# Keys and queries of the fifth unit turned by DMA, with the order of the work planned anew

## The chip, the cores and the metric

The kernel runs on one core of one Trainium2 chip. The metric is the time of the device in microseconds. The core has five engines that run side by side, each with an order of instructions of its own: TensorE (PE; its loads of weights are shown apart as PEld), VectorE (DVE), ScalarE (ACT), GpSimd (POOL) and SyncE (SP). Transfers run on 16 DMA engines; here nearly all of them are issued by SP, and the weights by POOL.

## The reference

The reference is a gated linear attention, followed by a feed-forward layer with an exact gelu. Batch 4, 8 heads, 768 tokens, 48 numbers a head; the feed-forward part has 3072 tokens, 384 columns and a hidden width of 2048.

```
f = sigmoid(f_logit)
for t in range(S):                       # per batch and head
    state = f[t][:, None] * state + outer(k[t], v[t])      # 48 x 48
    y[t] = q[t] @ state
x = y with heads side by side            # 3072 x 384
out = gelu(x @ w_in) @ w_out             # 384 -> 2048 -> 384
```

## The kernel before

**Tiles.** The tokens are cut into 24 tiles of 128 (n = 0 to 23), six to a batch. Two tiles make a unit (u = 0 to 11, n = 2u and 2u + 1). Units 0 to 4 are pair units: two neighbouring tokens lie on one partition, so that a load's runs are 384 bytes; units 5 to 11 have their tokens one to a partition.

**Attention, one unit.** SP loads the gate logits, k, q and v (L433 for pair units, L441 for others). ACT takes exp and ln of the gates (E and L, L478 and L481). PE sums the logarithms over a tile's tokens (C, L494 to L504), and ACT turns the sums into factors (L509, L511, and L514 or L518 for a whole tile's decay). DVE, in two cases POOL, multiplies k and q with them (L524, tile `sc`), and v is cast to bf16 (L529, on POOL unless the unit is in `HVC`). Then keys and queries have to be turned, so that the 48 numbers of a head lie on the partitions (function `turn`): either PE turns them into a PSUM bank in 8 transposes a tile (L557) and DVE, or ACT for tiles in `HKQ`, copies the bank to `kq` (L563), or, for units in `KDMA`, SP issues one DMA transpose for each tile (L545). PE forms scores (A: L723 in pair units, L661 in others), DVE masks them (L570). PE adds up the state's change (S: L745 or L684), which DVE and POOL carry on from tile to tile (L590, L594, L596, L601), and forms y from scores and from the state (L765, L644, L697, L638). y is cast (L614; ACT for tiles in `HYB`) and turned into x^T, by PE and a copy (L630, L633; ACT for tiles in `HX`) or by a DMA transpose (L618) for units in `XDMA`.

**Feed-forward, one group of 256 tokens, one for each unit.** F1: 48 products with w_in (L801), gelu of 512 columns at a time on ACT (L811); F2: 32 products with w_out, 16 for each of the two tiles, planned in pieces of 4 (L820), then a copy to SBUF (L834, on DVE for tiles in `ODVE`, else on ACT) and a store (L836). exp and ln lie in another table set than gelu, so ACT loads a table at each change between them (L865).

**The order.** Nothing is scheduled by hand or by the hardware across engines: the class `Plan` collects all operations with an expected duration, what they read and write, the buffers they need and a rank, and then places them one by one, always the one that could start first, with equal times (to 0.05 us) going by rank. That gives each engine a fixed order. The rank is 20 for each unit (10 for each tile) plus an offset by kind (`PRI`; feed-forward products come 1000 later), plus a random offset: one of at most 1.0 for all, and one from a generator for each unit, whose seed stands in `SEEDS` and whose width is 0.5, 1, 3 or 8, by the seed's remainder on division by 4. The loads go in the order of `LOADS`, where a letter and a number name one load of a unit (f0: gates of unit 0), u4 all four of unit 4, and i and o pieces of w_in and w_out. Buffers are limited too: four PSUM banks are for F1, F2 and what `EG`, `ET`, `EX` and `EA` put there, four for the attention. Until 30 us PE fills planned gaps with products of a junk tile (L859) that nobody reads.

Of the kernel before, what the change touches and what calls it, by code (L numbers as in the profile page):

```python
# [24 lines left out]

SPREAD, SEED = (1.0, 97)

SEEDS = [0, 3, 358, 3531, 1454, 1223, 983, 3849, 2582, 1403, 2107, 2867]

EAGER = 0.0  # L30

HOLD = 25.0
PRI = {'C': 0, 'T': 1, 'A': 2, 'S': 2.5, 'Y': 3, 'X': 4, 'F': 5}
BANKS = (4, 0, 4)


# [45 lines left out]
class Plan:  # L82
# [30 lines left out]
    def run(self):  # L113
        free = dict.fromkeys(list(LAT), 0.7)
        free["DMA"] = 1.8
        rng = random.Random(SEED)
        own = [random.Random(x) for x in SEEDS]
        for o in self.ops:
            if o.prio > -5:
                k = min(max(int(o.prio % 1000) // 20, 0), len(SEEDS) - 1)  # L120
                o.prio += rng.uniform(-SPREAD, SPREAD)
                if SEEDS[k]:
                    w = (0.5, 1.0, 3.0, 8.0)[SEEDS[k] % 4]
                    o.prio += own[k].uniform(-w, w)
# [84 lines left out]
EG = [0, 1]  # L209
ET = [0, 1]  # L210
EX = [0]
EA = []
SPLIT = []
HVC = []
HKQ = [0, 2]
HYB = [1]
HX = []
GKP, GQP = ([2], [3])
GAM = []
ODVE = [0, 1, 2, 3, 4, 5, 6, 7, 8, 9, 10, 11, 12, 13, 14, 15, 16, 17, 18, 19, 20, 21, 22, 23]  # L220
XDMA = [5, 6, 7, 8, 9, 10, 11]
KDMA = [5, 6, 7, 8, 9, 10, 11]
AJ = [2, 3, 4, 5, 6, 7, 8, 9, 10, 11]
NGT = 4
WARM = 30.0
LOADS = ['f0', 'k0', 'v0', 'q0', 'f1', 'v1', 'k1', 'q1', 'i0', 'k2', 'f2', 'v2', 'q2', 'i1', 'i2', 'i3', 'o0', 'o1', 'o3', 'f3', 'o2', 'k3', 'q3', 'v3', 'u4']
LOADS += [f"u{n}" for n in range(12) if f"u{n}" not in LOADS and f"c{2 * n}" not in LOADS and f"f{n}" not in LOADS]


@with_exitstack  # L230
def kernel(
# [181 lines left out]
    wo_src = moe_w_out.rearrange("(r p j) m -> r p j m", r=4, j=4)  # L413
    for what in LOADS:
        m = int(what[1:])
# [35 lines left out]
    def decays(u):  # L451
# [33 lines left out]
        for j, n in enumerate(ns):  # L485
# [36 lines left out]
            for w, nm, a, b, off in ((0, "kp", "kt", rg, 0), (1, "qp", "qt", gt, 1)):  # L522
# [4 lines left out]
                    port=True, name=f"{nm.upper()}{n}")  # L527
            hv = u in HVC
            P.add("ACT" if hv else "POOL", 0.40 if hv else 0.47, lambda y=y, j=j, hv=hv: (nc.scalar.copy if hv else nc.gpsimd.tensor_copy)(  # L529
# [5 lines left out]
    def copier(act):  # L535
        return nc.scalar.copy if act else nc.vector.tensor_copy

    def turn(u, kq):


        for j in range(2):
            n = 2 * u + j
            sc = X[n]["sc"]
            if u in KDMA:
                P.add("DMA", 1.5, lambda sc=sc, j=j: nc.sync.dma_start_transpose(  # L545
# [6 lines left out]
            def tpv(tp=tp):  # L552
                return tp.t().bitcast(BF16).rearrange("a (i p t) -> a i p t", i=2, p=P2)

            def trans(i, tpv=tpv, sc=sc):
                for p in range(P2):
                    nc.tensor.transpose(tpv()[:, i, p, :], sc.t()[:, i, 2 * p:2 * p + 2, :], ident)  # L557
            P.add("PE", 0.225, lambda trans=trans: trans(0), rd=[("kp", n), "ident"], wr=[("tk", n)],
                  bufs=[tp, sc, kq], prio=pr + PRI["T"], opens=tp, name=f"Tk{n}")
            P.add("PE", 0.225, lambda trans=trans: trans(1), rd=[("qp", n), "ident"], wr=[("tq", n)],  # L560
                  bufs=[tp, sc], prio=pr + PRI["T"], name=f"Tq{n}")
            help_ = n in HKQ
            P.add("ACT" if help_ else "DVE", 0.86 if help_ else 0.61, lambda tpv=tpv, j=j, help_=help_: copier(help_)(  # L563
                kq.t()[:, :, :, j, :].rearrange("a i p t -> a (i p) t"), tpv().rearrange("a i p t -> a (i p) t")),
                  rd=[("tk", n), ("tq", n)], wr=[("kq", n)], bufs=[tp, kq], prio=pr + PRI["T"], name=f"KQ{n}")

    def mask_scores(aps, ams, key, nm, rd, pr, mk, mkey):
        for hh in range(2):
# [3 lines left out]
                mk.unsqueeze(1).to_broadcast([C, P2, C]), ALU.mult),  # L572
                rd=[rd, mkey], wr=[key + (hh,)], bufs=[aps[hh], ams[hh]], prio=pr + PRI["A"], name=nm)

    def carry(n, sp, mm, mmdur, mmrd, mmbufs, first_c):
# [4 lines left out]
        if mm is not None:  # L580
            P.add("PE", mmdur, mm, rd=mmrd, wr=[("sp", n)], bufs=[sp, tn] + mmbufs + ([] if first_c else [rr]),
                  prio=pr + PRI["S"], opens=sp, name=f"S{n}")

        def spf():
            return sp.t()[:, 0:P2 * 96].rearrange("q (p e) -> q p e", p=P2)

        def glb():
            return gl.t()[:, n % 2, :].unsqueeze(2).to_broadcast([C, P2, 2 * D])
        if first_c:
            P.add("DVE", 0.475, lambda: nc.vector.tensor_tensor(tn.t(), spf(), glb(), ALU.mult),  # L590
                  rd=[("sp", n), ("gl", n)], wr=[("tn", n)], bufs=[sp, tn, gl], prio=pr + PRI["S"] - 0.5, name=f"R{n}")
        else:
# [14 lines left out]
    def outputs(n, yp):  # L607
# [4 lines left out]
        yb = U[u]["yb"]  # L612
        help_ = n in HYB
        P.add("ACT" if help_ else "DVE", 0.40 if help_ else 0.475, lambda: copier(help_)(yb.t()[:, i, :], yp.t()[:, 0:HD]),  # L614
# [10 lines left out]
        def xpv():  # L625
            return xp.t().bitcast(BF16)[:, 0:KO * C].rearrange("a (i t) -> a i t", i=KO)
# [4 lines left out]
        P.add("PE", 0.17, xmm, rd=[("yb", n), "ident"], wr=[("xp", n)], bufs=[yb, xp, xT], prio=pr + PRI["X"], opens=xp, name=f"XT{n}")  # L631
        hx = n in HX
        P.add("ACT" if hx else "DVE", 0.39 if hx else 0.27, lambda: copier(hx)(xT.t()[:, j], xpv()),  # L633
# [13 lines left out]
    def attn_nat(u):  # L647
# [3 lines left out]
        for j in range(2):  # L651
# [5 lines left out]
            def amm(j=j, aps=aps):  # L657
                for p in range(P2):
                    for hh in range(2):
                        r = slice(64 * hh, 64 * hh + 64)  # L660
                        nc.tensor.matmul(aps[hh].t()[:, p * C:(p + 1) * C], kq.t()[r, 0, p, j, :], kq.t()[r, 1, p, j, :],  # L661
                                         start=True, stop=True)
            if u in AJ:
                both.append((n, amm, aps, ams))
# [40 lines left out]
    def attn_pair(u):  # L705
# [8 lines left out]
        for jk in range(2):  # L714
            aps = [(s_fh if jk and u in EA else s_ap).new() for _ in range(2)]
            ams.append([s_am.new(), s_am.new()])

            def amm(jk=jk, aps=aps):
                for p in range(P2):
                    for cc in range(2):  # L720
                        for hh in range(2):
                            r, t = slice(64 * hh, 64 * hh + 64), slice(64 * cc, 64 * cc + 64)
                            nc.tensor.matmul(aps[hh].t()[t, p * C:(p + 1) * C].rearrange("a (j t) -> a j t", j=2),  # L723
                                             kq.t()[r, 0, p, jk, t], kq.t()[r, 1, p, :, t], start=True, stop=True)
            if u in AJ:
                both.append((jk, amm, aps, ams[-1]))
# [55 lines left out]
    def ffn_group(g):  # L782
# [31 lines left out]
        for s_ in range(s):  # L814
# [9 lines left out]
            if n == NCH - 1:  # L824
# [7 lines left out]
                continue  # L832
            od = n in ODVE
            P.add("DVE" if od else "ACT", 0.475 if od else 0.40, lambda op=op, osb=osb, od=od: copier(not od)(osb.t(), op.t()[:, 0:d_model]),  # L834
# [64 lines left out]
```

## Time and profile before

The time before is 184.66 us, the median of 3 runs (184.57 to 184.75). The profiled execution has a span of 183.4 us, with a granted TensorE clock of 0.997.

| | |
|---|---|
| PE busy | 173.3 us, 94% of the span |
| ACT busy | 122.0 us, 67% |
| DVE busy | 100.1 us, 55% |
| POOL busy | 55.2 us, 30% |
| F1 products (L801) | 576, 273 ns each from start to modelled end |
| F2 products (L820) | 384, 326 ns each |
| turns of keys and queries on PE (L557) | 80, for five units |
| DMA transposes of keys and queries | 14, for seven units, 3.2 us to landing |
| bytes read and written in HBM | 25.17 MB and 4.72 MB |

Matmuls are pipelined, so that their durations overlap: a matmul's share of PE's time is the distance from its start to the next one's. [...] A wait is named after what ended it.

### The profile page before, as it was taken

The numbers are of one execution on the slowest core, as the hardware profiler recorded it, in microseconds if no ns is written. First come the engines' busy times: TensorE is split into PE (matmuls) and PEld (weight loads), VectorE is DVE, ScalarE is ACT, GpSimd is POOL, SyncE is SP. The second block draws the span as 40 slices with busy tenths as digits, with TensorE's granted clock in tenths as the row PEclk, the third lists the DMA queues.
The fourth block names the chain that finished last, engine by engine and source line by source line (L and its number), as shares of the span: only waits on it lengthen the run. The fifth ranks groups of instructions, "written<-read, shape, count | busy, mean of one in ns | idle before, by whom it ended". The sixth has DMA issues, their size and how long they took to land.

```text
span 183.4 us, 4932 instructions
## 1 busy us (share of the span) xinstructions
PE 173.3 (94%) x2006; PEld 132.8 (72%) x2006; DVE 100.1 (55%) x193; ACT 122.0 (67%) x207; POOL 55.2 (30%) x118
## 2 busy tenths in 40 slices
PE   7687999999999998998999999999999999999991
PEld 2355679865778677977668987689876796998650
DVE  4288830068987698275978507746115896301111
ACT  2763299965487876989759777537899862495100
POOL 7758970005067342104065101160111830000000
PEclk9999999999999999999999999999999999999998
DMA  5999999989999999999899799998992873201021
GB/s 144 261 261 226 267 168 202 191 217 280 269 225 226 184 186 192 192 184 201 157 209 221 180 180 178 195 219 198 183 237 59 173 157 74 58 31 43 17 99 55
DMA packets 104821, 32.09 MB, mean 175 GB/s; under 512 B 99936, under 2 KB 103904, under 8 KB 104800
## 3 DMA queue, kind: packets, MB, share of 16 engines
q1 hardware_dynamic: 102880, 28.55, 72.6%
q0 software_dynamic: 1776, 3.15, 9.6%
q8 instruction: 15, 0.25, 0.5%
q10 hardware_dynamic: 144, 0.10, 0.2%
q14 instruction: 6, 0.05, 0.1%
HBM read 25.17 MB, written 4.72 MB: 163 GB/s over the span
## 4 chain that ended last, share of the span: by engine, by line
PE 66%; DMA 13%; SPq 10%; DVE 4%; ACT 3%; issue 2%; POOL 0%; DVEq 0%
PE ps L820 30%; PE ps L801 26%; DMA fl<-in_f_logit_dram 9%; SPq L433 6%; SPq L441 3%; DMA vt<-in_v_dram 2%; PE ps L661 2%; DMA kt<-in_k_dram 2%; PE ps L697 1%; ACT L865 1%; DVE sc L524 1%; PE ps L638 1%; PE ps L494 1%; ACT fl L478 1%; SPq L836 1%
## 5 line engine op out<-in xcount | busy, mean ns | idle before, releaser
L811 ACT ACTIVATE gT<-ps 128x512 bf16<-128x512 f32 x96 | 57.8, 672 | 20.8 <-PE ps L801 19.0
L801 PE MATMUL ps<-xT,win 128*128 128x256 bf16 x576 | 69.0, 273 | 0.6 <-ACT gT L811 0.6
L820 PE MATMUL ps<-wout,gT 128*128 128x384 bf16 x384 | 69.0, 326 | 0.0
L801 PEld LDWEIGHTS <-win 128*128 128x128 bf16 x576 | 61.3, 114 | 3.1 <-issue 0.7
L820 PEld LDWEIGHTS <-gT 128*128 128x128 bf16 x384 | 35.9, 98 | 20.3
L834 DVE COPY osb<-ps 128x384 f32<-128x384 f32 x23 | 12.6, 553 | 29.0 <-PE ps L820 18.9
L529 POOL CAST vb<-vt 128x384 bf16<-128x384 f32 x24 | 13.3, 566 | 49.5 <-DMA vt<-in_v_dram 49.3
L570 DVE TENSOR_TENSOR am<-ps,mask 128x512 bf16<-128x512 f32 x28 | 17.4, 681 | 11.3 <-PE ps L661 11.3
L524 DVE TENSOR_TENSOR sc<-qt,gt 128x384 bf16<-128x384 f32 x23 | 13.8, 616 | 17.1 <-ACT gt L511 16.6
L596 POOL TENSOR_TENSOR tn<-rr,gl 128x384 f32<-128x384 f32 x16 | 14.5, 904 | 24.9 <-ACT fl L478 14.6
L601 POOL CAST sb<-tn 48x192 bf16<-48x192 f32 x40 | 15.1, 377 | 18.2 <-DVE tn L590 6.8
L865 ACT ACT_TABLE_LOAD x15 | 19.2, 1283 | 0.3
L524 DVE TENSOR_TENSOR sc<-kt,rg 128x384 bf16<-128x384 f32 x23 | 14.4, 633 | 6.6 <-ACT rg L509 6.3
L509 ACT ACTIVATE rg<-ps 128x384 f32<-128x384 f32 x24 | 11.8, 499 | 8.6 <-PE ps L496 4.8
L614 DVE CAST yb<-ps 128x384 bf16<-128x384 f32 x23 | 12.3, 553 | 6.8 <-PE ps L697 3.6
L478 ACT ACTIVATE fl<-fl 128x768 f32<-128x768 f32 x12 | 10.2, 849 | 8.4 <-DMA fl<-in_f_logit_dram 8.3
L511 ACT ACTIVATE gt<-ps 128x384 f32<-128x384 f32 x24 | 11.7, 502 | 3.0 <-PE ps L500 3.0
L570 DVE TENSOR_TENSOR am<-ps,maskp 128x512 bf16<-128x512 f32 x20 | 12.5, 681 | 2.1 <-PE ps L723 2.1
L859 PE MATMUL ps<-junk 128*128 128x512 bf16 (+3 forms) x34 | 9.8, 418 | 1.6 <-POOL junk L851 1.3
L594 DVE TENSOR_TENSOR rr<-ps,tn 128x384 f32<-128x384 f32 x16 | 8.8, 551 | 3.4 <-POOL tn L596 1.2
L481 ACT ACTIVATE lf<-fl 128x768 bf16<-128x768 f32 x12 | 10.1, 845 | 0.3
L557 PE MATMUL ps<-ident,sc 128*128 128x128 bf16 x80 | 6.5, 220 | 1.3 <-POOL sc L524 0.8
(65 smaller groups left out, 122.6 us busy)
## 6 DMA issues: line engine op xcount, KB each, us to landing
out_dram<-osb SPq DMA_DIRECT2D x23, 192.0 KB, 2.9
fl<-in_f_logit_dram SPq DMA_DIRECT2D x14, 192.0 KB, 3.8
kt<-in_k_dram SPq DMA_DIRECT2D x14, 192.0 KB, 3.8
qt<-in_q_dram SPq DMA_DIRECT2D x14, 192.0 KB, 4.1
vt<-in_v_dram SPq DMA_DIRECT2D x14, 192.0 KB, 3.9
fl<-in_f_logit_dram SPq DMA_DIRECT2D x5, 384.0 KB, 5.9
kt<-in_k_dram SPq DMA_DIRECT2D x5, 384.0 KB, 6.3
vt<-in_v_dram SPq DMA_DIRECT2D x5, 384.0 KB, 6.1
```

The costliest lines, as they stand in the source:

```text
L478: nc.scalar.activation(v, v, AF.Exp, scale=-1.0)
L524: P.add("POOL" if pl else "DVE", 0.80 if pl else 0.475, lambda w=w, a=a, b=b, y=y, j=j, pl=pl: (nc.gpsimd if pl else nc.vector).tensor_tensor(
L529: P.add("ACT" if hv else "POOL", 0.40 if hv else 0.47, lambda y=y, j=j, hv=hv: (nc.scalar.copy if hv else nc.gpsimd.tensor_copy)(y["vb"].t ...
L570: P.add("POOL" if pl else "DVE", 1.15 if pl else 0.61, lambda hh=hh, pl=pl: (nc.gpsimd if pl else nc.vector).tensor_tensor(ams[hh].t(), ap ...
L596: P.add("POOL", 0.83, lambda: nc.gpsimd.tensor_tensor(tn.t(), rr.t(), glb(), ALU.mult), rd=[("rr", n), ("gl", n)], wr=[("tn", n)], bufs=[r ...
L601: P.add("POOL", 0.36, lambda hh=hh: nc.gpsimd.tensor_copy(sb.t()[64 * hh:64 * hh + D, :, D * hh:D * hh + D], tn.t()[64 * hh:64 * hh + D, : ...
L614: P.add("ACT" if help_ else "DVE", 0.40 if help_ else 0.475, lambda: copier(help_)(yb.t()[:, i, :], yp.t()[:, 0:HD]), rd=[("yp", n)], wr=[ ...
L801: nc.tensor.matmul(hps.t()[:, i * tok:(i + 1) * tok].rearrange("a (s t) -> a s t", s=s), col(fo)[:, kk, :], xT.t()[:, :, kk, :], start=(kk ...
L811: nc.scalar.activation(to, fr, AF.Gelu)
L820: nc.tensor.matmul(op.t()[:, 0:d_model], gT.t()[:, fo, s_ * C:(s_ + 1) * C], wout[fo // 4][:, fo % 4, :], start=(fo == 0), stop=(fo == FO ...
L834: P.add("DVE" if od else "ACT", 0.475 if od else 0.40, lambda op=op, osb=osb, od=od: copier(not od)(osb.t(), op.t()[:, 0:d_model]), rd=[(" ...
L865: nc.scalar.preload_act_table_set({"exp": "natural_log_exp_and_others", "gelu": "gelu_and_others"}[o.table])
```

## The change

Unit 4, the last of the pair units, joins the units whose keys and queries are turned by DMA (`KDMA`). This takes its 16 transposes from PE and two copies from DVE, and gives SP's queue two DMA transposes more. With it the order is planned anew: new seeds, other offsets by kind (the turns now rank after the scores, and x and y before both), unit 3's v is loaded after all of unit 4's inputs. Several small operations go to other engines: the v casts of unit 1 from POOL to ACT (`HVC`), the key and query copy of tile 6 (`HKQ`), the y cast of tile 5 (`HYB`), the x copy of tile 4 (`HX`) and the output copies of tiles 3, 5 and 15 (no more in `ODVE`) from DVE to ACT. The second scores of unit 0 take banks of the feed-forward part (`EA`), and the scores of unit 9's two tiles are formed apart (`AJ`, L661 in two steps instead of one).

```diff
-SEEDS = [0, 3, 358, 3531, 1454, 1223, 983, 3849, 2582, 1403, 2107, 2867]
+SEEDS = [0, 684, 383, 3363, 2427, 131, 74, 3619, 3555, 1021, 519, 3174]
...
-PRI = {'C': 0, 'T': 1, 'A': 2, 'S': 2.5, 'Y': 3, 'X': 4, 'F': 5}
+PRI = {'C': 0, 'T': 4, 'A': 3, 'S': 3.5, 'Y': 2, 'X': 1, 'F': 5}
...
-EA = []
+EA = [0]
 SPLIT = []
-HVC = []
-HKQ = [0, 2]
-HYB = [1]
-HX = []
+HVC = [1]
+HKQ = [0, 2, 6]
+HYB = [1, 5]
+HX = [4]
...
-ODVE = [0, 1, 2, 3, 4, 5, 6, 7, 8, 9, 10, 11, 12, 13, 14, 15, 16, 17, 18, 19, 20, 21, 22, 23]
+ODVE = [0, 1, 2, 4, 6, 7, 8, 9, 10, 11, 12, 13, 14, 16, 17, 18, 19, 20, 21, 22, 23]
 XDMA = [5, 6, 7, 8, 9, 10, 11]
-KDMA = [5, 6, 7, 8, 9, 10, 11]
-AJ = [2, 3, 4, 5, 6, 7, 8, 9, 10, 11]
+KDMA = [4, 5, 6, 7, 8, 9, 10, 11]
+AJ = [2, 3, 4, 5, 6, 7, 8, 10, 11]
...
-LOADS = ['f0', 'k0', 'v0', 'q0', 'f1', 'v1', 'k1', 'q1', 'i0', 'k2', 'f2', 'v2', 'q2', 'i1', 'i2', 'i3', 'o0', 'o1', 'o3', 'f3', 'o2', 'k3', 'q3', 'v3', 'u4']
+LOADS = ['f0', 'k0', 'v0', 'q0', 'f1', 'v1', 'k1', 'q1', 'i0', 'k2', 'f2', 'v2', 'q2', 'i1', 'i2', 'i3', 'o0', 'o1', 'o3', 'f3', 'o2', 'k3', 'q3', 'u4', 'v3']
```

## The prediction

> **What bounds the kernel now.** I read the page from the top: busy times, slices, the chain, the groups; then the timeline at the places where TensorE (PE) stood still.
>
> ```profile
> PE 173.3 (94%) x2006; PEld 132.8 (72%) x2006; DVE 100.1 (55%) x193; ACT 122.0 (67%) x207; POOL 55.2 (30%) x118
> ...
> PE   7687999999999998998999999999999999999991
> ...
> DMA  5999999989999999999899799998992873201021
> ```
>
> PE is at 9 tenths in nearly every slice after the fourth (about 23 us), the last slice apart. DVE, ACT and POOL are far from full over the whole span. The 16 DMA engines are about 90% busy until slice 30 (some 140 us) and then nearly free. So PE is the bound, with a saturated DMA system beside it for three quarters of the time.
>
> ```profile
> PE ps L820 30%; PE ps L801 26%; DMA fl<-in_f_logit_dram 9%; SPq L433 6%; SPq L441 3%; DMA vt<-in_v_dram 2%; PE ps L661 2%; DMA kt<-in_k_dram 2%; PE ps L697 1%; ACT L865 1%; DVE sc L524 1%; PE ps L638 1%; PE ps L494 1%; ACT fl L478 1%; SPq L836 1%
> ...
> L801 PE MATMUL ps<-xT,win 128*128 128x256 bf16 x576 | 69.0, 273 | 0.6 <-ACT gT L811 0.6
> L820 PE MATMUL ps<-wout,gT 128*128 128x384 bf16 x384 | 69.0, 326 | 0.0
> ...
> L557 PE MATMUL ps<-ident,sc 128*128 128x128 bf16 x80 | 6.5, 220 | 1.3 <-POOL sc L524 0.8 <-DVE sc L524 0.4
> L563 DVE COPY kq<-ps 128x1024 bf16<-128x1024 bf16 x8 | 5.4, 680 | 0.0
> ```
>
> Counted from start to start (ends overlap), a matmul of L801 takes 0.109 us and one of L820 0.162 us: 576 x 0.109 + 384 x 0.162 = 125 us of the 183.4 us span are the feed-forward part, which no edit touches. In the list of the chain, the pieces before 27 us are loads, the third unit's decays and the first gelu; from 27.3 us to 179.6 us they are mostly PE pieces, end to end. The time is therefore: the start until 27 us, all PE work after it, PE's stops, and 3.8 us of tail (last copy and store).
>
> The stops, from gaps between starts after 27 us: 0.28 us at 41.4, 0.20 at 54.3, 0.66 at 72.1 and 0.77 at 82.5, together 1.9; besides these only 0.10 to 0.15 us where PE changes between the 64-row products of the attention and full ones.
>
> ```profile
> 72.76 0.34 PE L630 MATMUL ps<-ident,yb 128*128 128x128 bf16 x3 [0.49 <-DVE yb L614]
> ...
> 80.35 0.85 ACT L478 ACTIVATE fl<-fl 128x768 f32<-128x768 f32 x1 [0.61 <-DMA fl<-in_f_logit_dram]
> 81.21 1.28 ACT L865 ACT_TABLE_LOAD   x1
> 82.51 1.94 ACT L811 ACTIVATE gT<-ps 128x512 bf16<-128x512 f32 x3
> 83.31 0.93 PE L801 MATMUL ps<-xT,win 128*128 128x256 bf16 x7 [0.62 <-ACT gT L811]
> ```
>
> The first stop is an order in which PE comes to a transpose before DVE has copied its source. The second is a load that came 0.61 us late for ACT, whose queue had a gelu behind it, whose bank PE wanted.
>
> And the start:
>
> ```profile
> 22.63 0.85 ACT L478 ACTIVATE fl<-fl 128x768 f32<-128x768 f32 x1 [3.01 <-DMA fl<-in_f_logit_dram]
> ...
> 25.66 2.54 ACT L811 ACTIVATE gT<-ps 128x512 bf16<-128x512 f32 x4
> ```
>
> The first gelu stands behind the third unit's exp and ln, which waited for its gate load.
>
> [...] one transpose of this form is 1024 packets of 256 B which keep the 16 engines 1.39 us, 262 KB / 1.39 us = 190 GB/s. [...]
>
> **The change part by part.**
>
> *Unit 4 turned by DMA.* PE loses 16 transposes (2 token tiles x 8), DVE two copies of 0.68 us, and two PSUM banks are not taken. From the chain:
>
> ```profile
> 39.02 0.45 PE ps L557 x8
> ```
>
> and another 8 at 47.1 took 0.55, so 16 cost PE 0.90 to 1.10 us; I take 0.9. They stood at 53 to 57 us, inside the packed stretch, so this is on the path. Added: two transposes on SP's queue.
>
> ```profile
> 67.02 3.05 SPq L545 DMA_TRANSPOSE kq<-sc  x2
> ...
> kq<-sc SPq DMA_TRANSPOSE x14, 3.2
> ```
>
> Each holds SP 1.3 us and lands 3.2 us after issue; unit 5's pair also made SP wait 1.3 us for its first source. Who waits for the result: unit 4's score products, at 67.9 in the old order, though its operands were copied by 58.0. With sources ready at about 56.3, SP's 2.6 us and 3.2 us to land (the second overlaps), the result is there by about 62: 6 us of slack, so I cost this wait at zero. What is queued behind: SP's loads for units 5 to 7. They come 2 x 1.39 = 2.8 us (DMA time) to 3.9 us (2 x 1.3 of issue plus the wait) later, if nothing else absorbs it. From group 5 on, an x tile is ready 7.7 to 14.6 us before its first L801 product (x5 at about 89.0, used at 96.7; x7 106.9 and 121.5), except the last two groups, planned with 1.3 and 1.9. So a lateness of 3 us costs PE nothing by way of x. By way of ACT it can: at 80.35 ACT stood at a load with gelus behind it. Bounds 0 and 2.8 us; I take 0, because the new order reckons with the two transposes and can put that exp later.
>
> *v of unit 3 behind all of unit 4's loads.* Unit 3's v was cast at 44.9, unit 4's at 50.9. v3 now lands near 50.9, and k4, q4, f4 each one load (about 1.4 us by SP's spacing) sooner. v3's first user, the state product, ran at 51.9, and its scores' use at 62.8. Cost 0 to 1 us; I take 0.
>
> *Copies moved to ACT.* Off DVE: one key/query copy (0.68; ACT's takes 1.01), one y cast (0.55; ACT 0.48), one x copy (0.35), output copies 3, 5 and 15 (0.55 each). With unit 4's two copies DVE loses 1.36 + 0.68 + 0.55 + 0.35 + 1.65 = 4.6 us, 4.0 of it before 90 us. DVE is busy 9.17, 8.59 and 8.52 us of the three stretches of 10 us from 40 to 70, so there it is nearly a bound, and x2 to x4 come only 1.9 to 2.8 us before use. ACT gets some 4.4 us (1.01 + 0.48 + 0.4 + 3 x 0.5 + 2 x 0.5 for unit 1's v casts), where it had 5.08, 7.75 and 7.05 us busy. The copies of 384 columns have no ACT row of this form; between 0.32 (192 columns) and 0.67 (512), I take 0.5. On PE's path neither counts directly; it makes the short stops less likely in that stretch.
>
> *Unit 0's second scores in the other banks, unit 1's v casts on ACT.* Unit 1's second token tile waits on POOL for casts (two, 0.95 us together) before a 1.30 us product, so unit 1's y comes up to 1 us sooner. It does not move the first gelu, pinned behind the gate load at 22.6. PE idled or ran fillers for 1.4 us between the first L801 at 21.0 and 27.1, so more early work mostly becomes more idling. Bounds 0 and 1.4; I take 0.
>
> *Unit 9's joint scores split.* One more change of product form on PE: 0.1 to 0.2 us lost; I take 0.1.
>
> *The new order.* All ranks (turns and scores later, y and x earlier) and random offsets are redrawn. Every wait of 1.9 us is open: bounds from all closed (-1.9) to new ones. I take 0.4 net gain, since the two long ones are accidents of order and lateness, and DVE gets room, while new accidents are as likely as old ones.
>
> Sum: 184.66 - 0.9 + 0.1 - 0.4 = 183.5.
>
> **The rivals.**
>
> *More than that.* PE's stops all close and the start gains: 184.66 - 0.9 + 0.1 - 1.9 - 0.5 = 181.5. For it: DVE's load before 90 us and x and y ranked first; against: the start hangs on the gate load, whose place in the queue is unchanged.
>
> *Given back.* The 0.9 us turns into waits: PE's order is fixed, and what it leaves becomes longer idling at the next gelu or y. 184.66 and nothing gained. For it: gelu pace (0.6 us a piece against 0.65 us of products) lets ACT set the pace in the gelu stretches, and ACT gets 4.4 us more; against: outside the shown stops PE waits for nothing.
>
> *Slower: the load stream is the bound before 90 us.* DMA was 1.05 busy from 70 to 80 and a load was late already. With 2.8 us more ahead of it, the gelus behind the exp are 2.8 us later and PE stops for about that: 184.66 - 0.9 + 2.8 = 186.6; half of it absorbed gives 185.2. I name 186.0. For it: the late load above. Against: x5 and later are early by 8 us and more, so the exp need not stand before the gelus.
>
> **How the numbers follow.** Forecast (183.5) 0.5, more 0.17, given back 0.12, slower 0.21. The 0.2% bounds are 184.29 and 185.03. Faster 0.67, same 0.12, slower 0.21. For eight in ten I cut about a tenth at each end: half of the "more" case lies under 182.0, and half of the slower one, which spreads from 185.2 to 186.6, over 185.6.
>
> **What would show it.** L557 at 64 instead of 80; 16 DMA transposes of kq; PE's busy share about the same over a shorter span; the stops at 72 and 82 gone or smaller; unit 4's score products not waiting for SP; the first gelu still at about 25.7; loads of units 5 to 7 landing some 3 us later without a stop of PE. Wrong if ACT waits for a gate load with gelus behind it, if a new stop of over 1 us stands between 40 and 90 us, or if the first gelu moves by more than 1 us.

## The result and the profile after

The changed kernel takes 183.01 us (182.69 to 183.82, six runs) against 184.62 us (184.11 to 184.75, six runs beside them): a ratio of 0.9924, interval 0.9903 to 0.9946. By the medians that is 1.6 us less, by the ratio 1.4. The forecast was 183.5, in a range of 182.0 to 185.6.

From the page of the changed kernel, the busy times and the slices:

```profile
PE 173.0 (95%) x1991; PEld 131.9 (73%) x1991; DVE 95.7 (53%) x185; ACT 126.2 (69%) x215; POOL 52.9 (29%) x116
...
PE   7889789999999999999999999999999999999992
...
DMA  6999999989999999899999999889999943702112
```

PE is busy for nearly as many microseconds as before, in a shorter span. DVE lost 4.4 us and ACT gained 4.2, as the moved copies should do. The chain, from the same page, and three of the groups (line, engine, operation, operands, count | busy, mean ns | idle before it):

```profile
PE ps L801 33%; PE ps L820 32%; DMA fl<-in_f_logit_dram 6%; SPq L433 6%; DMA xT<-yb 2%; PE ps L661 2%; PE ps L697 2%; PE ps L494 1%; PE ps L638 1%; PE ps L684 1%; PE ps L723 1%; PE ps L557 1%; PE ps L765 1%; PE ps L745 1%; PE ps L644 1%
```

```profile
L557 PE MATMUL ps<-ident,sc 128*128 128x128 bf16 x64 | 5.3, 220 | 0.5 <-DVE sc L524 0.4
...
L563 DVE COPY kq<-ps 128x1024 bf16<-128x1024 bf16 x5 | 3.4, 682 | 0.0
...
L563 ACT COPY kq<-ps 128x1024 bf16<-128x1024 bf16 x3 | 3.0, 1016 | 2.8 <-PE ps L557 1.6 <-DVE rr L594 1.2
```

There are 64 transposes instead of 80. Loads of v and k, which had 4% of the chain before, are gone from its list, and the chain's share on PE has grown from 66% to 79%.

Where the time went is read from PE alone. I take the distance from each matmul's start to the next one's, beginning with the 25th product of L801, from where these products run without a break; what goes beyond a matmul's usual distance is a stop. How the attention's products and the stops share their time depends on what is called usual; their sum hardly does. All in us:

| | before | after | difference |
|---|---|---|---|
| start until the unbroken stretch | 27.10 | 27.19 | +0.09 |
| L801 and L820 | 122.97 | 122.99 | +0.02 |
| turns of keys and queries (L557) | 2.72 | 1.83 | -0.89 |
| other attention products | 23.45 | 23.15 | -0.30 |
| stops and changes of form | 3.03 | 2.59 | -0.44 |
| after the last matmul | 3.76 | 3.57 | -0.19 |

The differences add up to -1.71 us; the spans differ by 183.4 - 181.7 = 1.7. The cause of the last row is not shown: the last copy and store are of another tile after the change, but two runs further down don't fit an explanation by that order: with the changed kernel's last stores and the turn on PE it is 3.69, with the old order and the turn by DMA 3.64.

The stops at 54, 72 and 82 us are gone. In their place the timeline of PE shows 0.33 us near 79 and this one:

```profile
140.47 1.47 PE L801 MATMUL ps<-xT,win 128*128 128x256 bf16 x12 [0.34 <-DMA xT<-yb]
```

PE now reaches the tenth group before its x has landed, where before the change that x was there some 13 us ahead. Counted as the prediction counted, by what the gaps of 0.2 us and more have beyond the usual distance, the stops were 1.9 us before (at 41, 54, 72 and 82 us) and are 1.1 after (0.30 at 42, 0.34 at 79, 0.51 at 140).

The start stands where it stood (ACT, timeline of the changed kernel; the first gelu is at 25.76 us, before the change it was at 25.66):

```profile
22.72 0.84 ACT L478 ACTIVATE fl<-fl 128x768 f32<-128x768 f32 x1 [4.21 <-DMA fl<-in_f_logit_dram]
23.60 0.85 ACT L481 ACTIVATE lf<-fl 128x768 bf16<-128x768 f32 x1
24.46 1.28 ACT L865 ACT_TABLE_LOAD   x1
25.76 3.13 ACT L811 ACTIVATE gT<-ps 128x512 bf16<-128x512 f32 x5
```

And the new transposes, on SP, with the first product of unit 4's scores on PE:

```profile
52.16 3.12 SPq L545 DMA_TRANSPOSE kq<-sc  x2
```

```profile
61.03 0.64 PE L723 MATMUL ps<-kq 64*64 64x128 bf16 x32
```

SP waited 0.64 us for the first source. With 3.3 us to landing the second is there at about 57.4; the scores come 3.6 us later and don't wait.

The gate loads behind these transposes did come later. The last one of unit 6 landed at 65.90 us before the change and lands at 69.16 after it. But ACT's exp of unit 6 now stands 9 us further on, 6.2 us behind the landing. First the kernel before, then the changed one:

```profile
66.43 0.88 ACT L478 ACTIVATE fl<-fl 128x768 f32<-128x768 f32 x1
```

```profile
75.39 0.90 ACT L478 ACTIVATE fl<-fl 128x768 f32<-128x768 f32 x1
```

Unit 7's last gate load lands sooner than before, at 76.79 instead of 80.33 us, ahead of its exp at 79.49; so the stop at 82 us, which came from that load, has nothing left to wait for.

### The profile page after: what moved, and what is told of

Read it like the earlier page. It is cut to its first block, busy times and chain, and to the rows that moved or that the text cites. A ratio compares the mean times of both kernels' runs of the same rounds, so it can differ in the third digit from the quotient of the medians.

```text
span 181.7 us, 4908 instructions
## 1 busy us (share of the span) xinstructions
PE 173.0 (95%) x1991; PEld 131.9 (73%) x1991; DVE 95.7 (53%) x185; ACT 126.2 (69%) x215; POOL 52.9 (29%) x116
## 4 chain that ended last, share of the span: by engine, by line
PE 79%; DMA 8%; SPq 6%; ACT 2%; DVE 2%; issue 1%; DVEq 0%; ACTq 0%
PE ps L801 33%; PE ps L820 32%; DMA fl<-in_f_logit_dram 6%; SPq L433 6%; DMA xT<-yb 2%; PE ps L661 2%; PE ps L697 2%; PE ps L494 1%; PE ps L638 1%; PE ps L684 1%; PE ps L723 1%; PE ps L557 1%; PE ps L765 1%; PE ps L745 1%; PE ps L644 1%
## 5 line engine op out<-in xcount | busy, mean ns | idle before, releaser
L811 ACT ACTIVATE gT<-ps 128x512 bf16<-128x512 f32 x96 | 58.4, 668 | 23.4 <-PE ps L801 21.8
L801 PE MATMUL ps<-xT,win 128*128 128x256 bf16 x576 | 68.6, 273 | 1.0 <-DMA win<-in_moe_w_in_dram 0.7
L820 PE MATMUL ps<-wout,gT 128*128 128x384 bf16 x384 | 68.3, 326 | 0.0
L801 PEld LDWEIGHTS <-win 128*128 128x128 bf16 x576 | 61.3, 114 | 3.5 <-DMA win<-in_moe_w_in_dram 1.0
L820 PEld LDWEIGHTS <-gT 128*128 128x128 bf16 x384 | 35.9, 98 | 20.9
L596 POOL TENSOR_TENSOR tn<-rr,gl 128x384 f32<-128x384 f32 x16 | 13.9, 870 | 43.1 <-DVE rr L594 23.3
L529 POOL CAST vb<-vt 128x384 bf16<-128x384 f32 x22 | 12.3, 572 | 43.6 <-DMA vt<-in_v_dram 43.4
L834 DVE COPY osb<-ps 128x384 f32<-128x384 f32 x20 | 11.1, 555 | 23.7 <-PE ps L820 17.6
L601 POOL CAST sb<-tn 48x192 bf16<-48x192 f32 x40 | 14.6, 364 | 12.1 <-DVE tn L590 6.5
L859 PE MATMUL ps<-junk 128*128 128x512 bf16 (+2 forms) x35 | 10.6, 437 | 1.8 <-POOL junk L851 1.3
L859 PEld LDWEIGHTS <-junk 128*128 128x128 bf16 x35 | 3.6, 113 | 5.9 <-issue 3.3
```

The costliest lines, as they stand in the source:

```text
L596: P.add("POOL", 0.83, lambda: nc.gpsimd.tensor_tensor(tn.t(), rr.t(), glb(), ALU.mult), rd=[("rr", n), ("gl", n)], wr=[("tn", n)], bufs=[r ...
L601: P.add("POOL", 0.36, lambda hh=hh: nc.gpsimd.tensor_copy(sb.t()[64 * hh:64 * hh + D, :, D * hh:D * hh + D], tn.t()[64 * hh:64 * hh + D, : ...
L801: nc.tensor.matmul(hps.t()[:, i * tok:(i + 1) * tok].rearrange("a (s t) -> a s t", s=s), col(fo)[:, kk, :], xT.t()[:, :, kk, :], start=(kk ...
L811: nc.scalar.activation(to, fr, AF.Gelu)
L820: nc.tensor.matmul(op.t()[:, 0:d_model], gT.t()[:, fo, s_ * C:(s_ + 1) * C], wout[fo // 4][:, fo % 4, :], start=(fo == 0), stop=(fo == FO ...
L859: nc.tensor.matmul(o.opens.t()[:, 0:w], junk[:, 0:C], junk[:, 0:w], start=True, stop=True, skip_group_check=True)
```

## The experiments

Times are compared as ratios to the kernel before, run beside each kernel. "Order kept" means that the plan is made as in the named kernel and only single operations are changed when it is written out, so that every engine has the same order but for these. Edits are given in short, not as code, unless they are a single setting.

**The changed kernel again.**

> The changed kernel once more, as the measure on this chip for the kernels run beside it: 0.9924 of the kernel before, 183.0.

Measured: 183.65 us (183.24 to 183.8), ratio 0.9951, interval 0.9931 to 0.9970. With the first measurement this says how far two measured ratios of one kernel lie apart: some 0.3%, or 0.5 us. The profiled spans of the two are 181.7 and 181.6 us. By this run the change is worth 0.9 us, by the first 1.4.

**The turn alone, in the old order (first try).**

```diff
-  PE: 16 transposes of unit 4; DVE: 2 copies to kq
+  SP: nc.sync.dma_start_transpose(kq..., sc...)   # at the place of the tile's query transposes
```

> The kernel before with its order kept on every engine; only unit 4's 16 transposes and two copies are left out of it, and two DMA transposes stand in SP's queue instead. Theory (PE's sum bounds): 0.9 us under the kernel before, 183.7. Rival one (the load stream bounds before 90 us): SP's loads for units 5 to 7 come some 3 us later, ACT stands at a gate load with gelus behind it, and the time is 184.6 to 186.5. Rival two (the gain of the change is its new order alone): 184.6.

Measured: 186.96 us, ratio 1.0130 (1.0109 to 1.0151). One of the transposes stood ahead of a source and turned old data, so a wait is missing here; the next run mends that.

**The turn alone, in the old order, behind both sources.**

> As the first try with the old order and the DMA turn, but each DMA transpose stands in SP's order behind both of its sources (in the first try one stood ahead of a source, so it turned old data). Theory (PE's sum alone decides): 183.7. Rival (load stream, as the first try showed with 187.0): ACT stands about 3 us at unit 6's gate load near 66 us, PE stops over 1 us near 70 us, and the time is 185.5 to 187.

Measured: 189.64 us (188.72 to 190.49), ratio 1.0286 (1.0256 to 1.0317): not 0.9 us less but 5.2 us more. The rival won, by more than it had forecast. PE's turns fell to 1.80 us as they should, and its stops rose from 3.03 to 8.75. Views of this kernel tell why, first SP's timeline, where a gap between rows is a wait in the queue (L200 is the transpose):

```profile
48.61 1.07 SPq L441 DMA_DIRECT2D qt<-in_q_dram  x1
54.31 1.33 SPq L200 DMA_TRANSPOSE kq<-sc  x1
55.69 0.56 SPq L836 DMA_DIRECT2D out_dram<-osb  x1
56.30 0.43 SPq L441 DMA_DIRECT2D vt<-in_v_dram  x1
```

```profile
SPq L200 <- DVE sc L524: 4.6, 1, 4.6
```

SP stood 4.6 us at the first transpose, until DVE had written its source. The windows show what the DMA engines did meanwhile (the last two columns are their share and GB/s):

```profile
45.00:50.00 5.00, 5.00 (x86) 3.54 (x85) 4.87 (x12) 2.61 (x6) 0.64 (x2) 1.00 1.17 272
50.00:55.00 5.00, 5.00 (x62) 4.00 (x60) 4.34 (x8) 4.48 (x9) 2.50 (x5) 1.00 0.35 72
```

They ran dry: a share of 0.35 instead of 1.17 (the packets' times added up, over 16 engines). The loads behind came late by that and by the transposes' own time, and the last to feel it were ACT at unit 6's gates and PE at the sums that need them:

```profile
72.28 0.84 ACT L478 ACTIVATE fl<-fl 128x768 f32<-128x768 f32 x1 [6.53 <-DMA fl<-in_f_logit_dram]
```

```profile
74.04 0.48 PE L494 MATMUL ps<-lf,trin 128*128 128x384 bf16 x1 [4.88 <-ACT lf L481]
```

Everything behind L494 in PE's order waited too, among it six feed-forward products that ran at once afterwards. Not all of the 5.2 us is waiting: after the stop PE's granted clock was 0.54 from 74 to 80 us, against 1.00 from 80 to 86. The 73 products from 74.0 to 79.6 us took 2.3 us more than their like elsewhere in this trace, of which 0.34 us is a wait that the kernel before has too; so some 2 us of the loss are, by this estimate, the clock.

**The turn put back on PE, in the new order.**

```diff
-  SP: 2 DMA transposes of unit 4
+  PE: 16 transposes, in two banks that are free at 57 to 60 us; DVE: 2 copies to kq
```

> The changed kernel with its order kept; only unit 4 is turned on PE again (16 transposes in two free banks, two copies on DVE, both before the scores need them), and its two DMA transposes are left out. Theory (PE's sum): 0.9 to 1.1 us over the changed kernel, 183.9 to 184.1. Rival (new order alone): 183.0. Rival (load stream): no slower than 183.0, or faster, since SP and the DMA engines lose two transposes.

Measured: 184.41 us (183.94 to 184.83), ratio 0.9986 (0.9972 to 1.0000), over the changed kernel's 0.9924 and 0.9951 by 0.6 to 1.1 us (the two were not run beside each other; the profiled spans are 182.7 and 181.7). PE's turns are 2.78 us, 0.95 more than in the changed kernel, and its stops hardly change (2.92). So in an order that has room for it, the turn is worth about what its transposes cost on PE, and without it the new order is at most 0.3% faster than the old one.

**The gate load of the third unit first.**

```diff
-  SP: ... k2, f2, v2, q2 ...
+  SP: ... f2, k2, v2, q2 ...          # order kept on all other engines
```

> The changed kernel with its order kept, but the gate load of the third unit changes places with its k load on SP. Theory (the start is pinned by that gate load): it lands about 1.4 us sooner, the first gelu starts at about 24.4 us instead of 25.8, and since PE had 1.4 us of fillers and stops there, the time falls by 0.8 to 1.3 us to 181.7 to 182.2. Rival (what is won at the start is lost at a later stop, because loads or gelus set the pace from there): under 0.3 us, 182.7 to 183.0.

Measured: 182.75 us (182.46 to 183.0), ratio 0.9893 (0.9874 to 0.9912), 0.6 to 1.1 us under the changed kernel. ACT's timeline:

```profile
21.02 0.84 ACT L478 ACTIVATE fl<-fl 128x768 f32<-128x768 f32 x1 [2.60 <-DMA fl<-in_f_logit_dram]
...
24.05 2.80 ACT L811 ACTIVATE gT<-ps 128x512 bf16<-128x512 f32 x4
```

The first gelu is 1.7 us earlier, the unbroken stretch begins at 26.38 instead of 27.19, and the last matmul ends 0.78 us earlier: what the start gives is carried to the end. The two were not run beside each other, and their ratios differ by little more than two measurements of one kernel do; but the profiled spans, 180.9 us against 181.7 and 181.6, say the same as the times. The rest of the 1.7 us PE spends on products that it has to do anyway and on fillers.

**The small copies back where they were, in the new order.**

```diff
-HVC = [1]; HKQ = [0, 2, 6]; HYB = [1, 5]; HX = [4]; 3, 5, 15 not in ODVE
+HVC = []; HKQ = [0, 2]; HYB = [1]; HX = []; all in ODVE      # when written out, not when planned
```

> The changed kernel with its order kept, but the small operations that moved to ACT are back on DVE and POOL (v casts of unit 1, key and query copy of tile 6, y cast of tile 5, x copy of tile 4, output copies 3, 5, 15), at the same places of the order. Theory (not on PE's path): within 0.3 us of 183.0. Rival (DVE's room between 40 and 70 us is what closed the stops at 54, 72 and 82 us): at least 0.7 us slower, 183.7 or more, with DVE over 8 of 10 us busy from 40 to 70 us.

Measured: 183.5 us (183.38 to 183.55), ratio 0.9938 (0.9922 to 0.9954), between the two measurements of the changed kernel. DVE is back at 9.12 us of the ten from 40 to 50 and at 9.11 of the next ten, and none of the three stops comes back (0.2 us near 48.7 and 0.3 us near 135 are new). The moves as such bring nothing that can be measured. Two things are not tested by this: their place in the plan, and DVE's room from 60 to 70 us, where DVE stays at 5.13 us, against 8.52 before the change.

**Without the filler near 26 us.**

```diff
-WARM = 30.0
+WARM = 24.0
```

> The changed kernel without the filler products near 26 us, nothing else. They wait for the bank of the first gelu and then take 0.65 us while a product for the same bank is ready. Theory: 0.65 us less, 182.4. Rival (gelu's pace sets the stretch after it, so that PE only waits there instead): 183.0.

Measured: 182.54 us (182.42 to 182.82), ratio 0.9905 (0.9887 to 0.9923), against 0.9951 (0.9931 to 0.9970) for the changed kernel, run beside it: 0.46%, 0.85 us, less, and 0.9 us less in the profile's span. So this version beats both kernels. In the changed kernel's first profile the filler takes from 26.55 to 27.19 us. It stands in PE's order behind the first gelu's release of a bank; without it the product begins there (PE's timeline):

```profile
26.34 3.87 PE L801 MATMUL ps<-xT,win 128*128 128x256 bf16 x34 [0.55 <-ACT gT L811]
```

Against the profile of the changed kernel taken beside it, the start gives 0.6 us of the 0.9. The other 0.3 come at the tenth group, where PE doesn't wait for x in this run; why it is there in time here is not shown.

**Both: gate load first and no filler.**

> The changed kernel with the third unit's gate load ahead of its k load and without the filler products near 26 us. With the load alone the stretch of feed-forward products began 0.8 us sooner and the profile's span fell by 0.8 us. Theory (start pinned, rest carried through PE): the filler takes 0.43 to 0.65 us of PE while products are ready, so 0.4 to 0.7 us under the run with the load alone, about 182.2. Rival (later waits take it back): 182.7.

Measured: 183.1 us (182.32 to 183.65), ratio 0.9925 (0.9902 to 0.9948), no better than either alone: the theory's sum failed. The stretch does begin at 25.91, 1.0 to 1.3 us earlier than in the two profiles of the changed kernel, and then meets two other waits:

```profile
30.45 0.74 PE L801 MATMUL ps<-xT,win 128*128 128x256 bf16 x5 [0.22 <-DMA win<-in_moe_w_in_dram]
```

```profile
140.29 1.47 PE L801 MATMUL ps<-xT,win 128*128 128x256 bf16 x12 [0.67 <-DMA xT<-yb]
```

The next piece of w_in is not there yet, and the tenth group's x lands at 140.25 us, nearly where it does in the changed kernel (140.43), though PE comes to it sooner. In the run without the filler alone it lands at 139.47; why not here is open.

**Unit 3's v ahead of unit 4's loads.**

```diff
-  SP: ... q3, f4, k4, q4, v4, v3 ...
+  SP: ... q3, v3, f4, k4, q4, v4 ...     # order kept on all other engines
```

> The changed kernel with its order kept, but unit 3's v load ahead of unit 4's four loads on SP, as before the change. Theory (v of unit 3 is not waited for, and the four others do not gain by coming sooner): within 0.3 us of the changed kernel. Rival (the four loads are what the DMA turn needs early: SP's two transposes wait 1.4 us longer for their sources and hold up the loads behind them, as in the old order): 0.7 us or more slower, with a stop of PE between 60 and 95 us.

Measured: 183.43 us (182.89 to 183.72), ratio 0.9941 (0.9921 to 0.9962): the same as the changed kernel, with no new stop.

**Planned anew: the old plan's settings with the turn, the new ones without it, and another draw.** The diffs are `KDMA = [4, 5, ...]` in the kernel before; `KDMA = [5, ...]` in the changed one; and `SEED` 98 instead of 97 in the changed one.

> The kernel before with unit 4 in the list of units turned by DMA, and its order planned anew with the old ranks, seeds, loads and engines. Theory (the turn pays once the order reckons with it): no stop of several us, 183.2 to 184.4. Rival (the new ranks, seeds and engines are needed as well): 184.6 or slower.

Measured: 193.45 us (192.19 to 194.81), ratio 1.0492 (1.0443 to 1.0540), the slowest of all, although this plan reckons with the two transposes. On SP's timeline four transposes hold the queue for 7.4 us, two more follow at 104.75, and ACT stands at the gate load behind those:

```profile
90.75 7.37 SPq L545 DMA_TRANSPOSE kq<-sc  x4
```

```profile
111.76 0.84 ACT L478 ACTIVATE fl<-fl 128x768 f32<-128x768 f32 x1 [6.77 <-DMA fl<-in_f_logit_dram]
```

PE's stops are 9.52 us, and that gate load is only one part of them. PE waits longer for DVE's masked scores, and then its granted clock is 0.67 from 112 to 120 us (the column before the last two in the windows):

```profile
109.60 0.27 PE L697 MATMUL ps<-vb,am 128*128 128x48 bf16 x4 [1.37 <-DVE am L570]
...
113.53 0.48 PE L494 MATMUL ps<-lf,trin 128*128 128x384 bf16 x1 [0.86 <-ACT lf L481]
```

```profile
105.00:112.00 7.00, 5.21 (x70) 3.26 (x69) 6.62 (x12) 0.24 (x1) 1.56 (x4) 0.89 1.13 172
112.00:120.00 8.00, 7.14 (x81) 5.60 (x80) 5.82 (x12) 6.56 (x13) 1.39 (x3) 0.67 1.12 222
```

How much of this the two new transposes cause is not shown. The theory of this run fell: planning with the turn is not enough.

> The changed kernel with unit 4 turned by PE, its order planned anew with the new ranks, seeds, loads and engines. Theory (PE's sum and a new draw of the stops): 183.7 to 185.0. Rival (the new ranks and engines carry the gain): 183.0.

Measured: 187.17 us (186.65 to 187.37), ratio 1.0144 (1.0122 to 1.0167). Against the changed kernel: 0.92 us of turns, 1.6 of stops (4.19), 0.7 in the other attention products, in which short stops are hidden. Neither guess had it so slow: with the turn on PE, the new settings give a plan that is slower than the old one.

> The changed kernel with another seed for the random offset of at most 1.0 that all operations get; nothing else is changed, the order is planned anew. Theory (every order has its own stops, and the seeds were drawn for this one): 0.3 to 2 us slower than the changed kernel, 183.3 to 185.0, by stops of PE of over 0.3 us at other places. Rival (the ranks and engines decide, not the draw): within 0.2 us.

Measured: 183.35 us (182.89 to 183.64), ratio 0.9940 (0.9920 to 0.9960): the same, though at 427 of the 1956 places in PE's order, fillers left out, the trace has a product of another line. So the gain doesn't hang on this one draw of the small offset. From this and the two runs before it I take that the settings of the plan and the set of operations have to fit each other; one other draw is too few to say how often an order is as good.

## Why the prediction was right, and where it was not

**PE's sum.** Said: 16 transposes, 0.9 us. Found: 0.89 in the trace of the change, 0.95 when they are put back in the new order. Right, and it is the largest term.

**The wait of unit 4's scores and v of unit 3.** Said: zero for both. SP waited 0.64 us, the scores not at all, with 3.6 us of slack where I had worked out 6; moving v3 back changes nothing. Right. (One reading on the way was off: x of unit 5 landed at 90.73 us in the kernel before, 6.0 us ahead of its use, not at about 89.0. Nothing hangs on it.)

**The loads behind the transposes.** Said: the loads come some 3 us later, at a cost of 0, between 0 and 2.8 us, because the new order reckons with the two transposes and can put the exp later. Found in the changed kernel: the transposes took 2.81 us of the DMA engines, as worked out; the second gate load of unit 5 and both of unit 6 landed 3.3 to 4.1 us later; and the exp of unit 6 stands 9 us later, so that nothing waited. Right for this kernel, in the value and, as far as the traces show, in where it comes from; no run moved that exp alone.

The upper bound was not right, nor is planning with the transposes enough. In the old order the same edit costs 5.2 us net, so over 6 us against the 0.9 it saves: I had bounded SP's wait by the 1.3 us of unit 5's pair, and it was 4.6, with the DMA engines dry behind it, and I had left out the clock, 0.54 from 74 to 80 us. And an order that reckons with the transposes can be worse still, as the 193.45 us show. That SP waits 0.64 us and not 4.6 has two parts in the traces: the first source is ready 2.2 us sooner (52.1 instead of 54.3), and SP comes to it 1.8 us later (51.5 instead of 49.7). Which of the settings does this is not settled: neither the copies' engines nor v3's place is it alone, and ranks and seeds were not tried one by one.

**Given back.** It did not come: both measurements of the changed kernel lie below the kernel before with their whole intervals.

**The slower rival.** Its mechanism, a gate load that comes late with work behind it on ACT, is what the runs in the old order show, to the engine and the line. It did not come about in the changed kernel.

**Copies moved to ACT.** Said: nothing directly. Found: nothing that can be measured, with them moved back. I also said that DVE's room made stops less likely; with DVE back at 91% from 40 to 60 us the three stops stayed away, so for that stretch the reason falls. From 60 to 70 us DVE has its room from the new order, and there it is not tested.

**The start.** Said: pinned by the third unit's gate load; the second scores of unit 0 and the casts of unit 1 cost nothing and win nothing. Found: unmoved in the change (+0.09), and 0.8 us sooner when that load goes first. Right; the scores and casts were not tried by themselves. I had missed that the filler near 26 us is part of the path: it was counted with the idling, but it takes 0.64 us, and without it the start gains 0.6.

**The stops.** Said: 0.4 net, from a guess, with the two long ones likely to go. They went, and two new ones came. Counted as in the prediction the net is 0.8, twice the guess; the 0.44 of the table comes near the guess only because its row holds the changes of form as well. The unit 9 split's 0.1 shows: from start to start the scores of L661 take 3.98 us after the change, 3.87 before, and have one exit more to another form. The 0.19 us at the very end were not foreseen, and their cause is open.

**The number.** The time lay 0.5 us under the forecast in the first measurement and 0.15 over it in the second. So near a hit is in part luck: the stops were undersized by 0.4 us, as much as two measurements of one kernel differ.

## What to carry to other kernels

Here one engine was full (PE, busy for 94% of the span before), and the 16 transposes taken from it were worth their distance from start to start, 0.89 us, in the order that kept feeding it; in the old order the same edit cost 5.2 us. So check the stops together with the sum. In the old order a DMA transpose waited 4.6 us for its source in a queue that also issues loads, and the exp of unit 6 behind it waited 6.5 us for its gates. So ask when the source is written before asking how long the transfer takes, and then where the first user of those loads stands in its engine's order: in the changed kernel 3.3 us cost nothing where the exp came 6.2 us after the landing. A filler that bridges planned idling can stand where a product could run: the one near 26 us took 0.64 us, and without it the time was 0.85 us less.

## What the runs showed of the hardware

After the stop of 4.88 us in the old order PE ran slow: the mean granted clock of the profiled execution is 0.982, and in the windows it is 0.54 from 74 to 80 us, where one matmul of L494 took 0.48 us instead of the 0.33 at 64.4 us in the kernel before (the column before the last two is the clock):

```profile
68.00:74.00 6.00, 1.17 (x11) 0.99 (x10) 2.31 (x4) 1.68 (x2) 1.29 (x2) 0.89 1.09 187
74.00:80.00 6.00, 5.62 (x81) 4.07 (x81) 1.94 (x4) 4.51 (x8) 1.19 (x3) 0.54 1.06 228
80.00:86.00 6.00, 6.00 (x52) 4.76 (x50) 2.09 (x5) 5.74 (x10) 1.20 (x3) 1.00 0.87 171
```

In the run that was planned anew with the old settings the clock was at 0.67 from 112 to 120 us, though no wait of PE just before was longer than 1.37 us; PE was busy for 5.21 of the 7 us to 112. In the first try, after a stop of 1.42 us by itself, the clock stayed up (mean 1.0). What sets it off is not shown by these three. I had not reckoned with it in mid-kernel.

For their bytes the DMA transposes are about as fast as the plain loads of units 5 to 11: in the trace of the kernel before, 1024 packets of 192 B, one load, keep the 16 engines 1.0 us, which is 195 GB/s, beside the 190 that the prediction worked out for a transpose.
